# First expert's first two units in thirds of 96 rows, the second weight block on another queue, and attention's first transfers joined

## The chip, the cores and the metric

One core of a Trainium2 chip runs the whole program. The metric is the device time of one execution in microseconds (us), the median of several runs. The engines are PE (matrix products, with its weight loads shown as PEld), DVE (vector work), ACT (activations and copies), POOL (GpSimd, here mostly for splitting weights and for issuing transfers) and SP (which only issues transfers). Each of them works through its own instructions in a fixed order and waits where an instruction's inputs or buffers aren't ready.

## The reference

```python
# attention: q, k, v are [4, 8, 576, 64]
scores = where(0 <= i - j < 64, q @ k.T / 8, -1e9)
x = softmax(scores) @ v                      # taken as x [2304, 512]
# mixture of 8 experts, 288 tokens each
order = argsort(-(x @ w_gate).flatten())     # 2304 * 8 logits
for idx in order:                            # greedy: a token goes to the best
    tok, e = idx // 8, idx % 8               # expert that has room for it
    if assigned[tok] < 0 and counts[e] < 288: assign(tok, e)
for e in range(8):
    y[assigned == e] = relu(x[assigned == e] @ w1[e]) @ w2[e]   # 512 -> 1024 -> 512
# dense layer: 512 -> 2048 -> 512
out = leaky_relu(y @ w_in, 0.01) @ w_out
```

## The kernel before

**Three stages share one instruction stream per engine.** `attention` (from L60) works through 18 blocks of 128 tokens: a mask product (L121) and the products of queries and keys (L130) into one accumulator, row maxima (L137), exponentials (L145), transposes (L150), products with the values (L165), and the gate logits (L93). Its first transfers go out one after another at the start: keys, queries, the transposed values for the gate, each by SP (L86, called from L203 to L223), and the constants by ACT's queue: the mask `maskb` (L1427), the 128 columns of `cbt` that the mask product multiplies with (L1428), and the identity `ident` (L1430). The gate's weights `wg_sb` go by SP (L1431).

`Router` finds each expert's 288 tokens. It is a chain of DVE steps and of small PE products (`rp<-r_oh,r_G`, 18 in a round, with one product by `r_sel` ahead and one by `pow` behind), phase 0 for the first expert. `Moe` then runs the experts: `gather_x` fetches an expert's 288 rows in three indirect transfers of 96 rows, issued by POOL; `xtrans(n, a)` turns one such third on PE (4 transposes, `xtp<-ident,xg`) and copies it to the tile `xT`; `hstep(i)` makes the products of one of eight units of the expert (`h<-xT,w_raw`, 4 products over 288 rows) and a relu on ACT (`hh<-h`); `ystep(i)` multiplies that with the second weights into accumulators (`ya<-hh,w_raw`). The first expert runs in plain float32, where one product shows as two records in the profile; the others run in two reduced parts. A unit's weights are one block of 512 KB (`w_raw` for the first expert), loaded by `load_raw`.

`Convert` prepares the dense layer's weights on the side. They lie in memory in an 8-byte form, as units `cv_in0` to `cv_in31` of 512 KB, and pass through four buffers `cv_in` in turn. Of each unit ACT makes `cv_r<-cv_in`, `cv_in<-cv_in` and `cv_in<-cv_r`, and a join on DVE (`cv_r<-cv_r,cv_in`) ends it; only then is the buffer free, and SP issues the next unit's transfer into it.

**What sets the order.** The program is written once, front to back, but the router's pieces and the conversions are put in between by a planner. `Clocks` keeps an estimated time for every engine, queue and tile; `RouteDriver.tick` and `until` ask it, at each place where they are called, which pieces of side work look ready by that estimate, and write these there. The result is a fixed order on every engine. All of these instructions are recorded through one helper, so they carry one line number (L1286), and the names of their tiles tell them apart.

**The place of the change** is the passage from the router to the first expert in `Moe.run` (from L1075). When the first expert's tokens are known, SP loads weight block 0 (`known`). POOL then issues the three gathers, weight block 1, the transfer of the conversion's unit 6, and weight blocks 2 to 7 (L1093 to L1099). PE runs 11 products on constants (`warm`) while the rows come in, then for each third the transposes and ACT's copy, with 4 further `warm` products behind the first third and 3 behind the last; then unit 0's four products over 288 rows (`hstep(0)`), and the loop over units.

Of the kernel before, what the change touches and what calls it, by code (L numbers as in the profile page):

```python
# [6 lines left out]
F32 = mybir.dt.float32  # L7
F32R = mybir.dt.float32r
BF = mybir.dt.bfloat16
# [31 lines left out]
def lay_wg(w):  # L41
    t = np.zeros((2, 64, 4, 2, 16), np.float32)
    for h in range(2):
        t[h, :, :, h, :8] = w.reshape(4, 2, 64, 8)[:, h].transpose(1, 0, 2)
    return t.reshape(128, 4, 32)
MW = 512
# [12 lines left out]
def attention(nc, tc, ident, identb, qT, kT, v, vT, wg_sb, maskb, xd, L, filler, early, late, done):  # L59


    with ExitStack() as ctx:
# [6 lines left out]
        def load_q(n):  # L69
            qb[n] = big.tile([128, 12, 64], F32, tag="aq", name=f"aq{n}", bufs=NQ)  # L70
            pend.append((qb[n].rearrange("p j c -> p (j c)"), qT[n]))
        def load_k(b, part):
            if part == 0:
                kb[b] = big.tile([128, 10, 4, 64], F32, tag="ak", name=f"ak{b}", bufs=2)
            c0, c1 = ((0, 4, 8, 10), (0, 5, 9, 10))[b % 2][part:part + 2]
            pend.append((kb[b][:, c0:c1].rearrange("p b u c -> p (b u c)"), kT[b, :, c0:c1].rearrange("p b u c -> p (b u c)")))
# [131 lines left out]
        early()  # L208
        load_q(1)
        load_k(0, 1)  # L210
# [68 lines left out]
def consts_np():  # L279

    f, i, b = {'ident': np.eye(128, dtype=np.float32)}, {}, {}
# [521 lines left out]
WARM = 11, 4, 3  # L803
class Moe:
    def __init__(self, nc, tc, ctx, ident, pp_misc, pa, pp, w12, wsp, xd, out, route):
# [12 lines left out]
        self.seq = seq  # L818
        self.raw, self.w, self.h, self.xg, self.xT, self.acc, self.ereg, self.ph, self.hdone = {}, {}, {}, {}, {}, {}, {}, {}, {}
# [78 lines left out]
    def xtrans(self, n, a):  # L898
        nc = self.nc
# [13 lines left out]
        if n == 0:  # L913
            nc.scalar.copy(hi[:, a].bitcast(F32), pt)
            return
# [4 lines left out]
    def hprod(self, i, hi):  # L920
# [3 lines left out]
        lo = self.hdone.get(i, 0)  # L924
        self.hdone[i] = hi
# [149 lines left out]
    def run(self):  # L1075
# [3 lines left out]
        def known():  # L1079
            self.conv.hold = True  # L1080
            self.load_raw(0)
# [12 lines left out]
        self.load_raw(1, nc.gpsimd)  # L1094
# [10 lines left out]
        warm(WARM[0])  # L1105
        self.split(0, 0)
        self.split(1, 0)
        self.split(0, 1)
        for a in range(3):
            R.until(nc.done(self.xg[0, a]))  # L1110
            self.xtrans(0, a)
            if a == 0:
                warm(WARM[1])
        R.until(nc.at["tensor"] + 600)
        warm(WARM[2])
# [254 lines left out]
def build(nc, tc, qT, kT, v, vT, wg, cfd, cid, cbd, w12, wio, out):  # L1370
    with ExitStack() as ctx:
# [3 lines left out]
        ident = c.tile([128, 128], F32, name="ident")  # L1375
        cft = c.tile([128, CFN - 128], F32, name="cft")
        cit = c.tile([128, CIN], I32, name="cit")
        cbt = c.tile([128, CBN - MW], BF, name="cbt")
        cf = {k: cft[:, o - 128:o - 128 + n] for k, (o, n) in CFO.items()}
        ci = {k: cit[:, o:o + n] for k, (o, n) in CIO.items()}  # L1380
        cb = {k: cbt[:, o - MW:o - MW + n] for k, (o, n) in CBO.items()}
        ones = c.tile([128, 128], BF, name="ones"); nc.vector.memset(ones, 1.0)

        nc.scalar.activation(ident[:, 0:1], ones[:, 0:1], AF.Exp)
# [39 lines left out]
        with tc.tile_pool(name="mk", bufs=1) as mk:  # L1424
            maskb = mk.tile([128, MW], BF, name="maskb")
            wg_sb = mk.tile([128, 4, 32], F32, name="wg_sb")
            nc.scalar.dma_start(maskb, cbd[:, :MW].bitcast(BF))  # L1427
            nc.scalar.dma_start(cbt[:, :128], cbd[:, MW:MW + 128].bitcast(BF))  # L1428
            def early():
                nc.scalar.dma_start(ident, cfd[:, :128])  # L1430
                nc.sync.dma_start(wg_sb, wg)  # L1431
            def late():
                nc.sync.dma_start(cit, cid)
                nc.sync.dma_start(cft, cfd[:, 128:])
                nc.sync.dma_start(cbt[:, 128:], cbd[:, MW + 128:].bitcast(BF))
                rt.start()
            attention(nc, tc, ident, cb['ident'], qT, kT, v, vT, wg_sb, maskb, xd, L, filler, early, late, done)
# [39 lines left out]
```

## Time and profile before

| | |
|---|---|
| time, median of 3 runs | 764.27 us (764.12 to 764.67) |
| the profiled execution's own time | 765.58 us |
| its span in the trace | 763.9 us |
| granted TensorE clock over the span | 0.984 of full speed |
| PE busy | 730.4 us, 96% of the span |
| PE weight loads busy | 616.5 us, 81% |
| DVE busy | 439.0 us, 57% |
| ACT busy | 338.3 us, 44% |
| POOL busy | 170.8 us, 22% |
| bytes moved by transfers | 138.55 MB, mean 181 GB/s |

The profile shows one execution, 1.31 us longer than the median, so sums made in its rows are carried over to the median as differences. Busy shares are means over three different stages: in 40 equal slices of the span PE is below nine tenths only in the first (start), in the fourth to the sixth (end of attention, and the router's first pick), and in the last. In the timeline a row gives a start, a length, the engine, the operation, and in square brackets the idle time ahead of it and what ended that; rows of one kind that follow each other are joined, with their count behind an x. In the rows of windows each engine has its busy time and its number of instructions, then come the mean granted clock, the busy share of the transfer engines, and GB/s.

### The profile page before, as it was taken

What the parts mean: (1) busy time and instruction counts of PE and PEld (TensorE: products, weight loads), DVE (VectorE), ACT (ScalarE), POOL (GpSimd) and SP (SyncE); (2) the same over time, 40 slices, a digit from 0 to 9 for tenths busy, and PEclk for the clock granted to TensorE, in tenths of its full rate; (3) what the DMA queues carried; (4) which work ended last, traced back from release to release, by engine and by line L of the source; (5) the groups of instructions that cost most, each with busy time, mean ns of one, the idle gap of its engine ahead of it and who ended that gap; (6) DMA issues with size and microseconds to landing.
All of it is one profiled execution on the core that took longest, in us unless ns stands there. A gap on an engine that the chain in (4) does not pass through costs nothing.

```text
span 763.9 us, 14821 instructions
## 1 busy us (share of the span) xinstructions
PE 730.4 (96%) x5680; PEld 616.5 (81%) x5681; DVE 439.0 (57%) x1120; ACT 338.3 (44%) x761; POOL 170.8 (22%) x263
## 2 busy tenths in 40 slices
PE   6989659999999999999999999999999999999996
PEld 4767537898877799977778899888889998888995
DVE  3798887888988896966659623322233232222332
ACT  4888806687766444422222454312245532222221
POOL 6262130500100052010000488000038830000201
PEclk9999769999999999999999999999999999999998
DMA  9996148733784654361324464533426462324652
GB/s 351 416 415 268 56 130 309 258 112 143 269 307 178 238 187 149 105 231 56 138 84 166 143 192 155 181 110 116 158 93 216 139 223 80 111 97 166 233 191 86
DMA packets 40088, 138.55 MB, mean 181 GB/s; under 512 B 4943, under 2 KB 5967, under 8 KB 40017
## 3 DMA queue, kind: packets, MB, share of 16 engines
q1 hardware_dynamic: 34992, 122.16, 44.6%
q0 software_dynamic: 4592, 15.21, 5.8%
q8 instruction: 45, 0.74, 0.4%
q10 hardware_dynamic: 432, 0.23, 0.1%
q14 instruction: 27, 0.21, 0.1%
HBM read 117.66 MB, written 19.92 MB: 180 GB/s over the span
## 4 chain that ended last, share of the span: by engine, by line
PE 90%; DVE 7%; ACT 1%; issue 1%; DMA 1%; POOLq 0%; POOL 0%; DVEq 0%; ACTq 0%
PE h L1286 40%; PE oa L1286 26%; PE ya L1286 14%; PE rp L1286 3%; PE ao L165 2%; PE apt L150 1%; PE as L130 1%; DVE r_G L1286 1%; DVE amx L137 1%; PE xtp L1286 1%; DMA cbt<-in_cb_dram 1%; PE rq L1286 1%; PE ag L93 1%; PE as L121 0%; DVE ax L181 0%
## 5 line engine op out<-in xcount | busy, mean ns | idle before, releaser
L1286 PE MATMUL h<-Y,w 128*128 128x512 f32 (+1 forms) x600 | 135.6, 372 | 0.0
L1286 PE MATMUL oa<-w,hh 128*128 128x512 f32 x540 | 133.5, 393 | 0.0
L1286 DVE SCALAR_TENSOR_TENSOR h<-h,tg 128x512 f32<-128x512 f32 (+1 forms) x80 | 51.6, 644 | 126.5 <-ACT tg L1286 126.1
L1286 ACT COPY tg<-h 128x512 f32<-128x512 f32 (+1 forms) x80 | 43.7, 547 | 171.3 <-PE h L1286 161.5
L1286 PEld LDWEIGHTS h<-Y,w 128*128 128x128 f32 x600 | 104.0, 189 | 18.3
L1286 PEld LDWEIGHTS oa<-w,hh 128*128 128x128 f32 x540 | 99.5, 188 | 19.7
L1286 POOL TENSOR_TENSOR w<-raw,w 128x512 fp32r<-128x512 f32 x50 | 63.0, 1292 | 194.2 <-ACT w L1286 193.9
L1286 PE MATMUL h<-xT,w 128*128 128x288 f32 x672 | 100.8, 297 | 0.1
L1286 PE MATMUL ya<-hh,w 128*128 128x288 f32 x672 | 100.4, 297 | 0.0
L1286 PEld LDWEIGHTS h<-xT,w 128*128 128x128 f32 x672 | 92.6, 188 | 0.9 <-DVE xT L1286 0.3
L1286 PEld LDWEIGHTS ya<-hh,w 128*128 128x128 f32 x672 | 92.1, 188 | 0.2 <-DVE hh L1286 0.2
L1286 PE MATMUL h<-Y,res 128*128 128x512 f32 (+1 forms) x360 | 84.4, 376 | 0.0
L1286 PE MATMUL oa<-res,hh 128*128 128x512 f32 x324 | 82.5, 399 | 0.0
L1286 DVE TENSOR_TENSOR hh<-h,hh 128x512 fp32r<-128x512 f32 (+1 forms) x80 | 51.0, 637 | 36.2 <-ACT hh L1286 33.4
L1286 ACT CAST hh<-h 128x512 fp32r<-128x512 f32 (+1 forms) x80 | 43.6, 545 | 62.9 <-DVE h L1286 62.4
L1286 POOL DMA_INDIRECT out_dram<-ot,sidx x18 | 22.5, 1251 | 218.2 <-DVE ot L1286 215.2
L1286 PEld LDWEIGHTS h<-Y,res 128*128 128x128 f32 x360 | 61.8, 188 | 11.3
L1286 PEld LDWEIGHTS oa<-res,hh 128*128 128x128 f32 x324 | 59.4, 188 | 13.3 <-ACT hh L1286 0.5
L1286 ACT ACTIVATE hh<-h 128x288 fp32r<-128x288 f32 (+1 forms) x64 | 26.6, 416 | 85.7 <-PE h L1286 78.0
L1286 ACT CAST w<-raw 128x512 fp32r<-128x512 f32 x112 | 64.2, 621 | 0.0
L1286 DVE SCALAR_TENSOR_TENSOR hh<-h,hh 128x288 fp32r<-128x288 f32 x56 | 25.5, 455 | 65.5 <-ACT hh L1286 62.0
L145 ACT ACTIVATE ap<-as,anm 128x128 f32<-128x128 f32 x144 | 42.0, 405 | 18.0 <-DVE anm L138 11.5
(177 smaller groups left out, 935.1 us busy)
## 6 DMA issues: line engine op xcount, KB each, us to landing
w<-wsp SPq DMA_DIRECT2D x80, 512.0 KB
raw<-in_w_dram SPq DMA_DIRECT2D x53, 512.0 KB
cv_in<-in_wio_dram SPq DMA_DIRECT2D x31, 512.0 KB
wsp<-w SPq DMA_DIRECT2D x20, 512.0 KB
avo<-in_v_dram SPq DMA_DIRECT2D x6, 876.0 KB
aq<-in_q_dram SPq DMA_DIRECT2D x12, 384.0 KB
avt<-in_vt_dram SPq DMA_DIRECT2D x6, 768.0 KB
xd<-ax SPq DMA_DIRECT2D x18, 256.0 KB
```

The source lines that it names most:

```text
L93: nc.tensor.matmul(ps[32 * u:32 * u + 32, :], wg_sb[:, u, :], vtb[m][:, u, :], start=True, stop=True, skip_group_check=True)
L130: nc.tensor.matmul(S[64 * t:64 * t + 64, a, u, :].rearrange("p (b c) -> p b c", b=2), q[h], k[h], start=False, stop=True, skip_group_check ...
L137: nc.vector.tensor_reduce(out=mx, in_=S[:, a:a + n], axis=AX.X, op=ALU.max)
L145: nc.scalar.activation(p[:, u, :], S[:, a, u, :], AF.Exp, bias=nm[a][:, u:u + 1], scale=0.125)
L150: nc.tensor.transpose(pt[:, u, :], p[:, u, :], ident)
L165: nc.tensor.matmul(o[64 * t:64 * t + 64, h // 4, h % 4, :], ptb[:, u, 64 * t:64 * t + 64], (ve, vo)[t][m][:, s, h, :], start=True, stop=Tr ...
L1286: return f(*a, **kw)
```

## The change

- **Attention's start.** Identity and gate weights come as one array `iwg` of 256 columns, in one transfer on ACT's queue; mask and the 128 constant columns of the mask product come as one tile and one transfer. SP's transfer of the gate weights is gone, and the second part of the first keys is issued ahead of the second queries.
- **Weight blocks 0 and 1** are both issued by SP in `known`; POOL's transfer of block 1 is gone.
- **Warm products.** The 4 and the 3 further ones are gone, the 11 stay.
- **Thirds.** The products of units 0 and 1 are no longer made over 288 rows at once. `third(i, a)` makes unit i's four products over the 96 rows of third a, as soon as these are turned: (0,0), (1,0) behind the second transposes, then after the third transposes (0,1), (1,1), (0,2), (1,2). ACT copies each third to a place of its own (`xF`), which the products read; for the first two thirds DVE copies the same transposes to `xT`, which the other six units read.

```diff
     t = np.zeros((2, 64, 4, 2, 16), np.float32)
...
-    return t.reshape(128, 4, 32)
+    return np.concatenate([np.eye(128, dtype=np.float32), t.reshape(128, 128)], 1)
...
         early()
+        load_k(0, 1)
         load_q(1)
-        load_k(0, 1)
...
-WARM = 11, 4, 3
+WARM = 11
...
         if n == 0:
-            nc.scalar.copy(hi[:, a].bitcast(F32), pt)
+            if a < 2:
+                x = lo if a == 0 else self.wk.tile([128, 2, 512], F32R, tag="hh", name="xF1")
+                self.xF[a] = x.bitcast(F32)[:, 0] if a == 0 else x.rearrange("p a n -> p (a n)").bitcast(F32)[:, :384].rearrange("p (k c) -> p k c", k=4)
+                nc.scalar.copy(self.xF[a], pt)
+                nc.vector.tensor_copy(hi[:, a].bitcast(F32), pt)
+            else:
+                nc.scalar.copy(hi[:, a].bitcast(F32), pt)
+                self.xF[a] = hi.bitcast(F32)[:, a]
             return
...
         lo = self.hdone.get(i, 0)
+        if lo == 12:
+            return
...
             self.conv.hold = True
-            self.load_raw(0)
+            for i in range(2):
+                self.load_raw(i)
...
         self.gather_x(0)
-        self.load_raw(1, nc.gpsimd)
...
-        warm(WARM[0])
+        warm(WARM)
...
+        def third(i, a):
+            if a == 0:
+                self.ph[i] = self.pp.tile([128, 512], F32, tag="h", name=f"h{i}")
+                self.hdone[i] = 12
+            for k in range(4):
+                nc.tensor.matmul(self.ph[i][:, 96 * a:96 * a + 96], self.w[i, 0][:, 128 * k:128 * k + 128], self.xF[a][:, k], start=(k == 0), stop=(k == 3), skip_group_check=True)
         for a in range(3):
             R.until(nc.done(self.xg[0, a]))
             self.xtrans(0, a)
-            if a == 0:
-                warm(WARM[1])
-        R.until(nc.at["tensor"] + 600)
-        warm(WARM[2])
+            if a < 2:
+                third(a, 0)
+        for i, a in ((0, 1), (1, 1), (0, 2), (1, 2)):
+            third(i, a)
+            R.tick()
         self.hstep(0)
...
-            nc.scalar.dma_start(maskb, cbd[:, :MW].bitcast(BF))
-            nc.scalar.dma_start(cbt[:, :128], cbd[:, MW:MW + 128].bitcast(BF))
+            maskb = mk.tile([128, MW + 128], BF, name="maskb")
+            nc.scalar.dma_start(maskb, cbd[:, :MW + 128].bitcast(BF))
...
             def early():
-                nc.scalar.dma_start(ident, cfd[:, :128])
-                nc.sync.dma_start(wg_sb, wg)
+                nc.scalar.dma_start(iwg, wg)
```

Since the planner's estimates move with the change, the order of side work moves too. Three places of it follow. In the names, `h0` and `h1` are the accumulators of units 0 and 1, `hh0` and `hh1` what the relu makes of them, `cv_in7` and `cv_r7` the conversion's unit 7 (read and made), and `rp` the router's products for the second expert.

On ACT, from the copies of the first expert's rows on, before:

```order
L1286 COPY xT0_0_2190<-xtp0_2_2231 128x384
L1286 ACTIVATE hh0_2280<-h0_2246 128x288
L1286 ACTIVATE cv_r6_2304<-cv_in6_2144 128x512
L1286 ACTIVATE cv_in6_2144<-cv_in6_2144 128x512
L1286 ACTIVATE hh1_2318<-h1_2282 128x288
L1286 CAST res_2_73<-cv_in4_1193 128x512
L1286 CAST res_3_74<-cv_in5_1196 128x512
L1286 ACTIVATE cv_in6_2144<-cv_r6_2304 128x512
L1286 ACTIVATE cv_r7_2379<-cv_in7_2269 128x512
```

and with the change:

```order
L1303 COPY xF1_2209<-xtp0_1_2204 128x384
L1303 COPY xT0_0_2187<-xtp0_2_2237 128x384
L1303 ACTIVATE cv_r7_2253<-cv_in7_2248 128x512
L1303 ACTIVATE hh0_2271<-h0_2196 128x288
L1303 ACTIVATE hh1_2273<-h1_2212 128x288
L1303 CAST res_2_73<-cv_in4_1190 128x512
L1303 ACTIVATE cv_r6_2301<-cv_in6_2132 128x512
```

The first activation of conversion unit 7 stood behind both relus and behind unit 6; now it stands ahead of them all, directly behind the copy of the last third.

On DVE, from the router's large r_G steps on, before:

```order
L1286 TENSOR_TENSOR r_G0_127<-r_m_1_2177,cit_64 128x6x127 x3
L1286 SCALAR_TENSOR_TENSOR r_E_1_0_2203<-r_M_122 128x18
L1286 SCALAR_TENSOR_TENSOR r_sat_126<-rp16_2211,ones_66 127x8
L1286 SCALAR_TENSOR_TENSOR r_G1_128<-r_E_1_0_2203,rp17_2238,cft_63 128x18x31
L1286 SCALAR_TENSOR_TENSOR r_E_1_1_2241<-r_E_1_0_2203,rp17_2238,r_M_122 128x18
L1286 SCALAR_TENSOR_TENSOR cv_r3_1781<-cv_r3_1781,cv_in3_1009 128x512
```

and with the change:

```order
L1303 TENSOR_TENSOR r_G0_127<-r_m_1_2174,cit_64 128x6x127 x2
L1303 COPY xT0_0_2187<-xtp0_0_2189 128x384
L1303 TENSOR_TENSOR r_G0_127<-r_m_1_2174,cit_64 128x6x127
L1303 SCALAR_TENSOR_TENSOR r_E_1_0_2202<-r_M_122 128x18
L1303 COPY xT0_0_2187<-xtp0_1_2204 128x384
L1303 SCALAR_TENSOR_TENSOR cv_r3_1778<-cv_r3_1778,cv_in3_1006 128x512
L1303 SCALAR_TENSOR_TENSOR r_sat_126<-rp16_2217,ones_66 127x8
```

The join of unit 3, behind which SP issues the transfer of unit 7, stood behind one router round (`r_sat`, `r_G1`, `r_E_1_1`); now it stands ahead of that round and behind the two new copies.

On PE, from the last transposes to the first product with the second weights, with the change:

```order
L1303 MATMUL xtp0_2_2237<-iwg_62,xg2_0_2130 128x96 x4
L1303 MATMUL h0_2196<-xF1_2209,w_raw0_2084 128x96 x4
L1303 LDWEIGHTS pow2_0_90
L1303 MATMUL rp17_2251<-r_sat_126,pow2_0_90 128x8
L1303 MATMUL h1_2212<-xF1_2209,w_raw1_2086 128x96 x4
L1303 MATMUL h0_2196<-xT0_0_2187,w_raw0_2084 128x96 x4
L1303 MATMUL h1_2212<-xT0_0_2187,w_raw1_2086 128x96 x4
L1303 MATMUL ya0_0_2275<-hh0_2271,w_raw0_2084 128x288
```

Before, `warm` and unit 0's four products over 288 rows followed the last transposes, with two rounds of the router's 18 products between the products of units 0 and 1; now nothing stands between the last third and `ya0`, and those two rounds come behind it.

## Rows read from the trace of the kernel before

**Rows 1.** The page's chain of work that ended last, by engine.
```profile
PE 90%; DVE 7%; ACT 1%; issue 1%; DMA 1%; POOLq 0%; POOL 0%; DVEq 0%; ACTq 0%
```
**Rows 2.** Windows: us, then PE, PEld, DVE, ACT, POOL busy, PEclk, DMA share, GB/s.
```profile
112.40:150.00 37.60, 37.60 (x294) 29.05 (x293) 30.46 (x88) 21.74 (x37) 11.30 (x26) 1.00 0.81 296
112.00:122.00 10.00, 10.00 (x111) 7.32 (x110) 7.48 (x17) 5.27 (x10) 1.16 (x3) 1.00 1.02 399
```
**Rows 3.** Waits of PE from 112.4 us to the end: total, times, longest.
```profile
PE rp L1286 <- ACT r_cq L1286: 0.8, 2, 0.6
```
**Rows 4.** Timeline of PE, 102 to 126 us: start, length, instruction.
```profile
108.63 0.52 PE L1286 MATMUL xtp<-ident,xg 96*128 96x96 f32 x4
108.99 1.03 PE L1286 MATMUL warm<-cbt 128*128 128x512 bf16 x4
...
113.03 0.59 PE L1286 MATMUL rp<-r_oh,r_G 128*128 128x8 bf16 x18
113.48 0.73 PE L1286 MATMUL h<-xT,w_raw 128*128 128x288 f32 x2
...
117.79 0.65 PE L1286 MATMUL ya<-hh,w_raw 128*128 128x288 f32 x2
```
**Rows 5.** Timeline of ACT, 102 to 126 us.
```profile
109.24 0.48 ACT L1286 COPY xT<-xtp 128x384 f32<-128x384 f32 x1 [13.76 <-PE xtp L1286]
...
115.33 0.41 ACT L1286 ACTIVATE hh<-h 128x288 f32<-128x288 f32 x1 [2.97 <-PE h L1286]
115.64 0.69 ACT L1286 ACTIVATE cv_r<-cv_in 128x512 f32<-128x512 f32 x1
...
121.40 0.69 ACT L1286 ACTIVATE cv_r<-cv_in 128x512 f32<-128x512 f32 x1 [0.65 <-DMA cv_in<-in_wio_dram]
```
**Rows 6.** Timeline of DVE, 102 to 126 us.
```profile
108.42 2.67 DVE L1286 TENSOR_TENSOR r_G<-r_m,cit 128x762 bf16<-128x762 f32 x3
111.01 0.17 DVE L1286 SCALAR_TENSOR_TENSOR r_E<-r_M 128x18 f32<-128x18 int32 x1
...
112.80 0.68 DVE L1286 SCALAR_TENSOR_TENSOR cv_r<-cv_r,cv_in 128x512 int32<-128x512 int32 x1
```
**Rows 7.** Timeline of SP's queue, 102 to 126 us: transfers issued.
```profile
102.76 0.36 SPq L1286 DMA_DIRECT2D w_raw<-in_w_dram  x1
113.51 10.58 SPq L1286 DMA_DIRECT2D cv_in<-in_wio_dram  x4
```
**Rows 8.** Timeline of POOL, 102 to 126 us: its last transfers issued.
```profile
110.00 3.17 POOL L1286 DMA_DIRECT2D w_raw<-in_w_dram  x6
```
**Rows 9.** Windows of 1 us, columns as in rows 2.
```profile
85.00:86.00 1.00, 0.00 (x0) 0.00 (x0) 0.93 (x4) 1.00 (x3) 0.00 (x0) 1.00 0.00 0
...
87.00:88.00 1.00, 0.27 (x4) 0.19 (x4) 0.82 (x4) 1.00 (x7) 0.00 (x0) 0.58 0.00 0
...
104.00:105.00 1.00, 0.66 (x19) 0.51 (x17) 0.24 (x1) 0.00 (x0) 0.00 (x0) 0.50 0.68 221
...
106.00:107.00 1.00, 1.00 (x4) 0.38 (x3) 0.87 (x4) 0.00 (x0) 0.70 (x2) 0.50 0.00 0
107.00:108.00 1.00, 1.00 (x5) 0.39 (x4) 0.97 (x6) 0.00 (x0) 0.69 (x2) 0.68 0.72 188
```
**Rows 10.** Groups of weight loads by line and form: busy, mean ns, idle before.
```profile
L1286 PEld LDWEIGHTS h<-xT,w_raw 128*128 128x128 f32 x64 | 11.4, 190 | 3.4 <-issue 0.4 <-ACT xT L1286 0.4
...
L93 PEld LDWEIGHTS ag<-avt,wg_sb 128*32 128x32 f32 x48 | 1.0, 113 | 3.5 <-ACT aptb L152 3.2 <-DMA avt<-in_vt_dram 0.3
```
**Rows 11.** Timeline of the first 12 us: ACT's queue, PE, PEld.
```profile
1.20 0.40 ACTq L1427 DMA_DIRECT2D maskb<-in_cb_dram  x1
1.63 0.45 ACTq L1428 DMA_DIRECT2D cbt<-in_cb_dram  x1
...
6.19 0.64 PE L121 MATMUL as<-maskb,cbt 64*64 64x512 bf16 x4 [6.19 <-DMA cbt<-in_cb_dram]
...
10.95 0.20 PEld L93 LDWEIGHTS ag<-avt,wg_sb 128*32 128x32 f32 x8 [0.33 <-DMA avt<-in_vt_dram]
```

More of the change, by code (lines that the diff above doesn't have):

```diff
@@ L279, in consts_np @@
 def consts_np():
-    f, i, b = {'ident': np.eye(128, dtype=np.float32)}, {}, {}
+    f, i, b = {}, {}, {}
     p = np.arange(128, dtype=np.float32)[:, None]
@@ L818, in __init__ @@
         self.seq = seq
+        self.xF = [None] * 3
         self.raw, self.w, self.h, self.xg, self.xT, self.acc, self.ereg, self.ph, self.hdone = {}, {}, {}, {}, {}, {}, {}, {}, {}
@@ L1374, in build @@
         dr = ctx.enter_context(tc.tile_pool(name="dr", bufs=1, space=bass.MemoryType.DRAM))
-        ident = c.tile([128, 128], F32, name="ident")
-        cft = c.tile([128, CFN - 128], F32, name="cft")
+        iwg = c.tile([128, 256], F32, name="iwg")
+        ident = iwg[:, :128]
+        cft = c.tile([128, CFN], F32, name="cft")
         cit = c.tile([128, CIN], I32, name="cit")
-        cbt = c.tile([128, CBN - MW], BF, name="cbt")
-        cf = {k: cft[:, o - 128:o - 128 + n] for k, (o, n) in CFO.items()}
+        cbt = c.tile([128, CBN - MW - 128], BF, name="cbt")
+        cf = {k: cft[:, o:o + n] for k, (o, n) in CFO.items()}
         ci = {k: cit[:, o:o + n] for k, (o, n) in CIO.items()}
-        cb = {k: cbt[:, o - MW:o - MW + n] for k, (o, n) in CBO.items()}
+        cb = {k: cbt[:, o - MW - 128:o - MW - 128 + n] for k, (o, n) in CBO.items() if o > MW}
         ones = c.tile([128, 128], BF, name="ones"); nc.vector.memset(ones, 1.0)
-        nc.scalar.activation(ident[:, 0:1], ones[:, 0:1], AF.Exp)
+        nc.scalar.activation(iwg[:, 0:1], ones[:, 0:1], AF.Exp)
         L = c.tile([128, 160], F32, name="L")[:, :NT * 8].rearrange("p (c e) -> p c e", e=8)
@@ L1424, in build @@
         with tc.tile_pool(name="mk", bufs=1) as mk:
-            maskb = mk.tile([128, MW], BF, name="maskb")
-            wg_sb = mk.tile([128, 4, 32], F32, name="wg_sb")
-            nc.scalar.dma_start(maskb, cbd[:, :MW].bitcast(BF))
-            nc.scalar.dma_start(cbt[:, :128], cbd[:, MW:MW + 128].bitcast(BF))
+            maskb = mk.tile([128, MW + 128], BF, name="maskb")
+            nc.scalar.dma_start(maskb, cbd[:, :MW + 128].bitcast(BF))
+            wg_sb = iwg[:, 128:].rearrange("p (u e) -> p u e", u=4)
             def early():
-                nc.scalar.dma_start(ident, cfd[:, :128])
-                nc.sync.dma_start(wg_sb, wg)
+                nc.scalar.dma_start(iwg, wg)
             def late():
                 nc.sync.dma_start(cit, cid)
-                nc.sync.dma_start(cft, cfd[:, 128:])
-                nc.sync.dma_start(cbt[:, 128:], cbd[:, MW + 128:].bitcast(BF))
+                nc.sync.dma_start(cft, cfd)
+                nc.sync.dma_start(cbt, cbd[:, MW + 128:].bitcast(BF))
                 rt.start()
-            attention(nc, tc, ident, cb['ident'], qT, kT, v, vT, wg_sb, maskb, xd, L, filler, early, late, done)
+            attention(nc, tc, ident, maskb[:, MW:], qT, kT, v, vT, wg_sb, maskb, xd, L, filler, early, late, done)
         pa = ctx.enter_context(tc.tile_pool(name="m_pa", bufs=4, space=PSUM, reuse_waits="tile"))
```

## The prediction

> **What bounds the kernel now.** Read the chain of work that ended last first: PE carries 90% of it [rows 1]. A share is a mean, so the next view is the windows. From 112.4 to 150 us PE is busy for all of its 37.60 us at full clock, with ACT at 21.74 and DVE at 30.46 us beside it [rows 2], and the table of waits says that this goes on: from 112.4 us to the end PE waits for another engine twice, 0.8 us in all [rows 3]. So whatever moves the point at which the first expert is under way moves the end by as much, and nothing behind it can take a delay up. What the change touches lies ahead of 112.4 us or directly behind it; the questions are when PE can begin `ya` (unit 0's second product), and with how much of the other work already done.
>
> Before, that product begins at 117.79 [rows 4]. By then PE has also done two router rounds that the change puts behind it. A round's 18 products put off the product behind them by 113.48 - 113.03 = 0.45 us [rows 4]; with the one by r_sel and the one by pow I take 0.5, so the two are 1.0 and the mark to compare with is 117.79 - 1.0 = **116.8**.
>
> **The change part by part.**
>
> *Thirds.* 16 records of 288 columns become 48 of 96, in six thirds of 8. No row has this product. The nearest is the transposes of the same 96 columns: four, and the next instruction begins 108.99 - 108.63 = 0.36 later [rows 4], so 90 ns a record. The other end is a limit by the weight load: a load of 32 columns takes 113 ns and one of 128 takes 190 [rows 10], a slope of 0.80 ns a column, so 103 ns for 128 columns. I take 90 (same columns) and keep 103. Third (0,0) can start when ACT's copy ends, 109.24 + 0.48 = 109.72 [rows 5]. Then 0.72 for a third, 0.36 for the transposes: (0,0) ends at 110.5, the second transposes at 110.8, (1,0) at 111.55, the router's group at 112.05, the third transposes at 112.4, (0,1) at 113.1, then the product by pow, which waits for DVE (below) until 113.15, (1,1) at 113.9, (0,2) at 114.65, (1,2) at **115.4**; at 103 ns it is 116.0. The relu of unit 0 (0.41, [rows 5]) fits beside (1,2). Standing alone, this part gives 1.4 us, or 0.8.
>
> *ACT's new order.* But the relu isn't next on ACT: the first activation of conversion unit 7 now stands ahead of both relus, and it waits for a transfer. That transfer goes into the buffer of unit 3, so SP issues it only when DVE's join of unit 3 has ended: before, the join ran from 112.80 for 0.68 [rows 6], and the issue stood at 113.51 [rows 7]. ACT got the data at 121.40, having waited 0.65 us for it with nothing else to do [rows 5]: 7.9 us for 512 KB. The reason is in the windows: from 112 to 122 us the transfer engines are 1.02 busy at 399 GB/s [rows 2], because POOL issued six weight blocks from 110.00 to 113.17 [rows 8] (block 1 and unit 6 lie ahead of them in its queue). Before, that lateness cost nothing, since both relus stood ahead; with the change PE's `ya` stands behind the relu, the relu behind the activation, and the activation behind this transfer.
>
> When is the issue now? DVE's three r_G steps take 0.89 each from 108.42 [rows 6]; the first copy to `xT` goes in behind the second, the second behind r_E. I price a copy at 0.48, as ACT's of the same tile [rows 5]; the other end is 0.68, the join of 512 columns [rows 6]. That puts the third r_G's end at 111.6, r_E's at 111.75 and the second copy's at 112.3, the join's at **113.0** and the issue with it (113.2 at the dear price), and the router's next step just behind. One block less is in POOL's queue, since block 1 goes by SP, right behind block 0. If the transfer lands when the whole backlog is through, one block less is 524 KB / 399 GB/s = 1.3 us off the 121.36 of before: 120.05. If it takes 7.9 us again, 120.9. I take the middle, **120.4**. The lowest price is that of a block with the engines to itself: block 0, issued at 102.76 [rows 7], and the engines idle in 106 to 107 [rows 9], so in by 106.0, 3.24 us, which would be 116.2.
>
> From 120.4 on: activation 0.69, relu 0.41 [rows 5], and 0.1 for the two handovers, so `ya` starts at **121.6**. Against 116.8 that is **+4.8 us**. PE has its last third behind it at 115.4 to 116.0 and nothing in its order to fill the gap: five to six us idle.
>
> *The clock in that gap.* The trace has one such gap: PE is busy 0.00 in 85 to 86, and the granted clock falls in 87 to 88 to a mean of 0.58 [rows 9], that is, to the lower level (0.50, 1.2 GHz) for most of it. Coming back, PE is at work again in 104 to 105 (0.66 busy, clock 0.50), and the clock rises in 107 to 108: a mean of 0.68 puts it at 107.64 [rows 9], 2.6 to 3.6 us later. I expect a fall inside the gap, and 2.8 us of work at half pace behind it: half of that, **+1.4**. Bounds: 0, if it stays; 2.8, if it takes twice as long to return.
>
> *Attention's start.* PE's first instruction waits until 6.19 for `cbt`, whose transfer is issued at 1.63, 0.43 behind the mask's at 1.20 [rows 11]. Joined, the bytes can land up to 0.43 sooner. But the gate's first load still waits 0.33 us at 10.95 for values that lie behind the same bytes [rows 11], and these don't shrink. Bounds -0.43 and 0; I take **-0.2**.
>
> *At nothing.* The 7 `warm` products run where PE waits anyway, and the thirds take their place as work that keeps the clock up. DVE's two copies matter only by the join's date, counted above. Weight block 1 on SP begins beside block 0 in a stretch at 0.68 of the engines' time [rows 9] and is needed at 110.8, so up to 0.3 on the gathers, covered by the gap. Router rounds run later, with the same wait as cover; were that gone, their 1.0 is already in the mark of 116.8.
>
> **Sum.** 4.8 + 1.4 - 0.2 = +6.0. The profiled execution's own time, 765.58, becomes 771.6; the median lies 1.31 below it, so the forecast for the median is 764.27 + 6.0 = **770.3**.
>
> **The rivals.**
>
> *The same stall, clock stays up.* For it: PE is busy until the gap at full clock, and the gap is shorter than the thin stretch behind 85 us. Against: the clock fell there some 2 us after PE stopped. 764.27 + 4.8 - 0.2 = 768.9.
>
> *Queues take turns.* If SP's queue got half of the engines as soon as it has work, unit 7 would need the 3.24 us of a lone block plus once more its own 1.3 us: in at 117.55, `ya` at 118.75, +1.95 - 0.2, the gap too short for the clock: 766.0. The trace speaks against it, since with a backlog of this kind the transfer took 7.9 us. The Trainium skill's page "DMA: Bandwidth & Descriptors", section "Queues, rings and completion order", states this rule (each engine goes round the queues that have work, a packet at a time); the 7.9 us don't agree with equal shares.
>
> *Not slower: unit 7 lands as a lone block would.* With one block less in POOL's queue and unit 6 first in it, the backlog might be thin at 113.0. In at 116.2, `ya` at 117.4, +0.6 - 0.2: 764.7. The point that decides: the sum stays within 0.2% if `ya` starts by 118.5, so if unit 7 lands by 117.3. For it: block 0's 3.24 us. Against: even with block 1 gone, the six blocks behind it were issued in the 3 us just ahead.
>
> *Faster: ACT is not held at all.* If unit 7 is in by 114, or the activation isn't where the order has it, the thirds bring their 1.4 at 90 ns, and with the start's 0.2 it is 762.7; at 103 ns 763.3, which is no change. Landing 1 us after its issue is against every row.
>
> **How the numbers follow.** A measurement of this kernel can tell about 0.2%, 1.53 us: faster is below 762.74, slower above 765.80. Chances: forecast 0.60; stall without the clock 0.20; taking turns 0.05; lone block 0.10; ACT not held 0.05. The first three are slower, 0.85; the fourth no change, 0.10; the last faster, 0.05. Range: up, the dear copies and 120.9 for the landing (+0.7) and a slower return of the clock, of which I take in most, 772.9. Down, it goes through the stall without the clock (768.4 at the early landing) and taking turns to 766.0. That leaves out the last two rivals, 0.15, and a little above.
>
> **What would show it.** Right: on ACT, `cv_r<-cv_in` directly ahead of the first `hh`, released by a transfer near 120.4 after some 7 us of idle; PE idle from about 115.5 to 121.6; the granted clock at 0.50 in a window behind that, products there at twice their length; the thirds' records at 90 to 103 ns. Wrong: that transfer landing by 117 (first step of the ACT part), a first `ya` ahead of 118.5, a gap on PE that another instruction fills, or a clock of 1.00 through the gap; and a delay that doesn't reach the end, which would mean that PE has slack behind 150 us that the waits don't show.

## The result, and the profile after

The changed kernel takes **771.11 us** (median of 6 runs, 770.33 to 772.66), against 764.47 (764.12 to 764.95, 6 runs) for the kernel before on the same chip: 1.009 times, 95% interval 1.0077 to 1.0103, or 6.6 us slower. Forecast were 770.3 and a range of 766.0 to 772.9. The profiled execution is the shortest of the six (770.33, span 768.7), so its rows show a loss of 4.7 against the span of before, and 1.9 us of the median's 6.6 are not in them: 0.8 because it is the shortest, 1.1 because the one of before was long.

ACT's timeline after the change (start, length, instruction, idle ahead of it and what ended that; this holds for all timelines below) answers to [rows 5]:

```profile
112.41 0.48 ACT L1303 COPY xT<-xtp 128x384 f32<-128x384 f32 x1 [1.26 <-PE xtp L1303]
119.15 0.66 ACT L1303 ACTIVATE cv_r<-cv_in 128x512 f32<-128x512 f32 x1 [6.26 <-DMA cv_in<-in_wio_dram]
119.71 0.69 ACT L1303 ACTIVATE hh<-h 128x288 f32<-128x288 f32 x2
```

The activation of unit 7 stands directly behind the third copy, waits 6.26 us for its transfer, and both relus come out behind it. DVE and SP, as [rows 6, 7]:

```profile
109.63 0.94 DVE L1303 TENSOR_TENSOR r_G<-r_m,cit 128x762 bf16<-128x762 f32 x1
110.49 0.17 DVE L1303 SCALAR_TENSOR_TENSOR r_E<-r_M 128x18 f32<-128x18 int32 x1
111.19 0.56 DVE L1303 COPY xT<-xtp 128x384 f32<-128x384 f32 x1 [0.53 <-ACT xF L1303]
111.66 0.68 DVE L1303 SCALAR_TENSOR_TENSOR cv_r<-cv_r,cv_in 128x512 int32<-128x512 int32 x1
```

```profile
112.37 0.34 SPq L1303 DMA_DIRECT2D cv_in<-in_wio_dram  x1
```

From issue to the activation it is 119.15 - 112.37 = 6.78 us. PE, as [rows 4]:

```profile
109.18 1.13 PE L1303 MATMUL h<-xT,w_raw 128*128 128x96 f32 x8 [0.61 <-ACT xT L1303]
110.14 0.49 PE L1303 MATMUL xtp<-iwg,xg 96*128 96x96 f32 x4
110.48 1.06 PE L1303 MATMUL h<-xT,w_raw 128*128 128x96 f32 x8
...
114.08 1.95 PE L1303 MATMUL h<-xT,w_raw 128*128 128x96 f32 x16
120.16 1.33 PE L1303 MATMUL ya<-hh,w_raw 128*128 128x288 f32 x2 [4.12 <-ACT hh L1303]
...
123.00 2.08 PE L1303 MATMUL ya<-hh,w_raw 128*128 128x288 f32 x4
124.92 0.65 PE L1303 MATMUL h<-xT,w_raw 128*128 128x288 f32 x2
```

PE has its last third behind it at 116.03 and waits 4.12 us. Then the first two records of `ya` (one product) take 1.33 us, where [rows 4] has 0.65. The windows of that stretch (columns as in [rows 2]) say why:

```profile
117.00:118.00 1.00, 0.00 (x0) 0.00 (x0) 0.00 (x0) 0.00 (x0) 0.00 (x0) 0.97 1.03 422
118.00:119.00 1.00, 0.00 (x0) 0.00 (x0) 0.00 (x0) 0.00 (x0) 0.00 (x0) 0.50 1.04 422
...
123.00:124.00 1.00, 1.00 (x4) 0.82 (x3) 0.79 (x2) 0.98 (x1) 0.00 (x0) 0.50 0.00 0
124.00:125.00 1.00, 1.00 (x4) 0.70 (x3) 1.00 (x4) 0.00 (x0) 0.00 (x0) 0.62 0.04 8
```

The granted clock falls to its lower level at 117.9, two us into the gap, and is back at 124.8 (0.62 in the last window), so PE works 4.6 us at 1.2 GHz. From the first `ya` to the next unit's first product it takes 124.92 - 120.16 = 4.76 us. All this time the transfer engines are full at 422 GB/s until the backlog is through.

How unit 7's transfer lands is told by the packets of the queues (`q0` is POOL's queue, `q1` SP's; packets, MB, share of the 16 transfer engines): first from its issue at 112.37 to its first packet at 115.88, then 115.9 to 118.4 us, then 118.8 to 122:

```profile
q0 software_dynamic: 373, 1.36, 100.2%
...
q0 software_dynamic: 146, 0.53, 52.2%
q1 hardware_dynamic: 130, 0.51, 50.1%
...
q0 software_dynamic: 200, 0.69, 52.7%
```

For 3.5 us nothing of it moves; then it gets as much as the backlog, 0.51 MB against 0.53; and it is through with 0.69 MB of the backlog still to come. The last weight block, issued at 111.03 and so ahead of it, lands at 122.0, behind it. In all twelve profiles with the weight blocks ahead of it (all but c2's, below) the first packet comes 3.4 to 3.6 us after the issue, and POOL's queue moves 1.25 to 1.46 MB in that time. What the transfer waits for then isn't shown.

The waits of PE from 112.4 us to the end (total, times, longest), as [rows 3]:

```profile
PE ya L1303 <- ACT hh L1303: 4.1, 1, 4.1
PE oa L1303 <- ACT hh L1303: 0.2, 1, 0.2
```

Nothing behind takes the delay up. The start, PE's timeline as [rows 11], and one row of before for the gate's products:

```profile
4.88 0.64 PE L121 MATMUL as<-maskb 64*64 64x512 bf16 x4 [4.88 <-DMA maskb<-in_cb_dram]
...
10.75 0.85 PE L93 MATMUL ag<-avt,iwg 128*32 128x384 f32 x8 [0.76 <-DMA avt<-in_vt_dram]
```

```profile
10.96 1.37 PE L93 MATMUL ag<-avt,wg_sb 128*32 128x384 f32 x8
```

The first product starts 1.31 sooner, the gate 0.21 sooner, and its eight records take 0.85 where they took 1.37: the first record of the granted clock in the trace, at 1.00, begins at 8.7 us here and at 12.1 before.

For what follows, one table read from PE's timelines of all profiled executions: **a** is the start of the router's last large group ahead of the first expert (`rp<-r_lo,r_OB`), **b** goes from a to the first `ya`, **c** from a to the start of the first expert's last `ya` record, **d** from that to the end of the span. The sum a + c + d is the end.

| kernel | a | b | c | d |
|---|---|---|---|---|
| before | 103.80 | 13.99 | 45.98 | 614.10 |
| changed | 102.74 | 17.42 | 52.32 | 613.54 |
| a1, units 6 to 8 held | 102.80 | 13.55 | 45.98 | 618.52 |
| a2, gap filled | 102.53 | 18.39 | 51.29 | 614.46 |
| a3, start alone | 102.80 | 13.99 | 45.98 | 613.05 |
| a4, start and block 1 | 102.64 | 14.15 | 46.14 | 613.20 |
| c1, activation behind relus | 103.33 | 12.77 | 50.21 | 614.44 |
| c2, less backlog | 102.67 | 15.01 | 47.92 | 613.56 |
| c3, before with the stall | 103.64 | 19.39 | 53.34 | 613.45 |
| c4, planner with one stream | 102.86 | 13.72 | 46.69 | 622.84 |
| c5, activation further back | 103.33 | 13.84 | 46.67 | 615.89 |
| d1, 96 columns in place | 103.69 | 15.36 | 47.37 | 613.86 |
| e1, thirds in before's order | 103.36 | 14.98 | 47.69 | 614.13 |

In the profile the change makes a shorter by 1.06, c longer by 6.34 and d shorter by 0.56. So all that is lost is lost within the first expert, and in the trace it is the gap and the slow products behind it. Whether the thirds have a part in it, the trace alone doesn't say.

### The profile page after: what moved, and what is told of

It reads as the page before. It is cut to its first block, busy times and chain, and to the rows that moved or that the text cites. A ratio compares the mean times of both kernels' runs of the same rounds, so it can differ in the third digit from the quotient of the medians.

```text
span 768.7 us, 14869 instructions
## 1 busy us (share of the span) xinstructions
PE 732.2 (95%) x5706; PEld 619.1 (81%) x5706; DVE 440.3 (57%) x1124; ACT 337.1 (44%) x761; POOL 165.6 (22%) x260
## 4 chain that ended last, share of the span: by engine, by line
PE 89%; DVE 7%; DMA 1%; ACT 1%; issue 1%; POOLq 0%; POOL 0%; SPq 0%; DVEq 0%; ACTq 0%
PE h L1303 39%; PE oa L1303 26%; PE ya L1303 14%; PE rp L1303 2%; PE ao L165 2%; PE as L130 1%; PE apt L150 1%; DVE amx L137 1%; PE xtp L1303 1%; DVE r_G L1303 1%; DMA cv_in<-in_wio_dram 1%; DMA aq<-in_q_dram 1%; PE warm L1303 1%; PE rq L1303 1%; ACT ap L145 1%
## 5 line engine op out<-in xcount | busy, mean ns | idle before, releaser
L1303 POOL DMA_INDIRECT out_dram<-ot,sidx x18 | 18.9, 1050 | 310.0 <-DVE ot L1303 134.7
L1303 POOL TENSOR_TENSOR w<-raw,w 128x512 fp32r<-128x512 f32 x48 | 60.4, 1295 | 95.4 <-ACT w L1303 95.0
L1303 POOL DMA_INDIRECT xg<-xd,r_ids x24 | 24.1, 1005 | 127.5 <-issue 48.6
```

The costliest lines, as they stand in the source:

```text
L1303: return f(*a, **kw)
```

## The experiments

The theory: one instruction, unit 7's activation ahead of the first relu, holds PE until a transfer lands, and the clock falls meanwhile. The rival: the thirds cost it (reloaded weights, DVE's copies, the order that comes with them), and the activation is only where the wait shows.

**a1: conversions held back.**

```diff
-                if n < 32 and (self.left[n] if n in self.out else ...
+                if n < 32 and n not in self.skip and (self.left[n] if n in self.out else ...
...
+        self.conv.skip = {7, 8}
...
+            if i == 1:
+                self.conv.skip = set()
```

> The changed kernel with one thing undone: ACT may not begin conversion units 6, 7 and 8 ahead of the first relu (6 may run behind it, 7 and 8 behind the second), so the activation that waits for unit 7's transfer stands behind both relus again. Stall theory: PE's gap of 4.1 us ahead of the first ya goes, and with it the 2.2 us that the first ya group lost at half clock (4.76 us from its first product to the next unit's, against 2.61 before): some 6.5 us less than the changed kernel in one profile, and against the kernel before the 1.06 us of the earlier start less what the thirds cost (120 ns a record in the trace of the change: they end 0.3 later than the mark 116.8 - 1.06): 763.7. Rival (the thirds' reloads, block 1 beside the gathers or DVE's copies are the cost, and the activation is only where the wait shows): another wait takes its place and the time stays above 768.

Measured: 767.73 (767.23 to 769.13; before 764.75; 1.0042, 1.0028 to 1.0055), neither 763.7 nor above 768. Ahead of the first relu `skip` is {6, 7, 8}. The gap is gone (b 13.55) and the first expert ends at 45.98, exactly as before; but d is 618.52. The planner, asked at other moments, laid out the rest anew, and PE meets waits there that neither kernel has (waits of PE in a1):

```profile
PE rp L1306 <- ACT r_cq L1306: 2.1, 1, 2.1
PE ya L1306 <- DVE hh L1306: 0.7, 1, 0.7
```

So 767.7 says nothing on the thirds: the edit changed more than it meant to. The runs c1, c2, c3 and c5 therefore move instructions behind the planner's back: it is told of them in the old place, and every other instruction keeps its order.

**a2: warm products in the gap.**

```diff
             R.tick()
+        for _ in range(16):
+            nc.tensor.eng.matmul(wt, self.warm[:, :128], self.warm, start=True, stop=True)
         self.hstep(0)
```

> The changed kernel, with 16 warm products (0.22 us each, 3.5 us in all) on PE behind the last third, in the gap; the gap's end stays set by unit 7's transfer. Clock theory: the granted clock stays at 1.00, the first ya group takes 2.6 us in place of 4.8, and the time falls by 2.2 to some 768.9; the stall of 4.4 us stays. Rival (the long products come from contention or from something else that ends with the transfer): no change against the changed kernel, 771.1.

Measured: 770.55 (769.6 to 772.6; 1.0085, 1.0069 to 1.01), only 0.6 below the change. PE and ACT in its profile:

```profile
115.47 3.40 PE L1134 MATMUL warm<-cbt 128*128 128x512 bf16 x15
120.91 0.75 PE L1305 MATMUL ya<-hh,w_raw 128*128 128x288 f32 x2 [2.04 <-ACT hh L1305]
...
123.63 0.65 PE L1305 MATMUL h<-xT,w_raw 128*128 128x288 f32 x2
```

```profile
119.91 0.66 ACT L1305 ACTIVATE cv_r<-cv_in 128x512 f32<-128x512 f32 x1 [7.62 <-DMA cv_in<-in_wio_dram]
```

The first `ya` group takes 123.63 - 120.91 = 2.72 us in place of 4.76, so the clock's part is 2.0 us, as the theory had it: the granted clock stays at 1.00 here. But the transfer, issued at 111.76, took 8.15 us here against 6.78, which gives 1.4 back in these two profiles. The landing varies between executions; that fits the wider runs here (3 us from lowest to highest) and in the change (2.3, against 0.9 in a3), though c3's four runs, which wait for it too, lie within 1.1. In the medians the clock's part is thus not separated from that.

**a3: the start alone**, the change's edits to the constants and attention's transfers and no others.

> The kernel before with attention's start alone from the change (identity with gate weights, mask with its constants, keys ahead of queries). If the 1.06 us by which the router's last products stood earlier in the profile of the change are all from here and reach the end: 763.4. If the gate's wait takes them back, as the prediction had it: 764.3.

Measured: 763.97 (763.53 to 764.39, 11 runs; before 764.75; 0.9992, 0.9983 to 1.0001): 0.8 gained in the medians, between the two expectations; the interval just takes in no change. In its profile a is 1.00 shorter.

**a4: start and block 1 on SP**, as a3, and with SP issuing weight block 1 and conversions held as in a1; units 0 and 1 over 288 rows.

> As the first run of this set, but with units 0 and 1 as products over 288 rows as before, and the 4 and 3 further warm products: what is left of the change is the start and block 1 on SP. Stall theory: 763.4, like the start alone (block 1 on SP is worth nothing by itself). The difference of the first run of this set to this one is the thirds' own price: +0.3 by the 120 ns a record of the profile; -0.8 to -1.4 by the 90 to 103 ns of the prediction.

Measured: 763.87 (763.3 to 764.64, 11 runs; 0.9989, 0.998 to 0.9998), like a3: block 1's queue and the held conversions are worth nothing that these runs can tell. The comparison with a1 fails, as a1's d shows.

**c3: the stall alone, in the kernel before.** One instruction is moved:

```diff
+        if i == 0:
+            self.conv.pre = self.conv.room(7)
+            nc.scalar.eng.activation(self.conv.pre, self.conv.st[7][:, :, 1].bitcast(F32), AF.Copy, scale=float(2.0 ** -112))
         if kind == "e" and n == 0:
             nc.scalar.activation(hi.bitcast(F32), ph[:, :N], AF.Relu)
```

> The kernel before with one instruction moved: the first activation of unit 7 stands ahead of the first relu on ACT, nothing else of the change. Stall theory: ACT gets the data at 121.4 as before, the relu ends at 122.4, ya starts at 122.5 in place of 117.8 (+4.7) and the clock falls in a gap of 4.8 us (+2.2): 764.75 + 6.9 = 771.6, all of the change's loss and its 0.8 gain at the start. Rival (the thirds are needed for the loss): +4.7 at the most, 769.5 or less.

Measured: **771.88** (771.01 to 772.12; before 764.6; 1.009, 1.0075 to 1.0104). ACT and PE in its profile:

```profile
122.02 0.66 ACT L974 ACTIVATE cv_r<-cv_in 128x512 f32<-128x512 f32 x1 [9.17 <-DMA cv_in<-in_wio_dram]
122.58 0.39 ACT L1292 ACTIVATE hh<-h 128x288 f32<-128x288 f32 x1
```

```profile
117.22 1.22 PE L1292 MATMUL h<-xT,w_raw 128*128 128x288 f32 x4
123.03 1.33 PE L1292 MATMUL ya<-hh,w_raw 128*128 128x288 f32 x2 [4.59 <-ACT hh L1292]
```

The old products, the old queues, the old start, and one activation in front of one relu: 7.3 us slower, with the same gap and the same slow products as in the change (c +7.36). The thirds aren't needed for a loss of this size.

**c1: that activation put back behind the two relus, in the changed kernel.**

```diff
+        if k == 0 and n == 7:
+            e, a, kw = self.nc.scalar, (o, t[:, :, 1].bitcast(F32), AF.Copy), dict(scale=float(2.0 ** -112))
+            e.clocks.charge(e.e, "activation", a, kw)
+            self.held = lambda: e.eng.activation(*a, **kw)
...
                     self.hstep(i + 1)
+                if i == 0:
+                    self.conv.held()
```

> The changed kernel with one instruction moved and every other one in its order on every engine: the first activation of unit 7 stands behind the two first relus on ACT, not ahead of them. Stall theory: no gap on PE ahead of ya, which starts at 116.1 in the profile (120.2 with the change), the clock stays up, and the gain is the stall and the clock together, 4.1 to 5.4 (the landing varied from 6.8 to 8.1 us) plus 2.2: some 764.0. Rival from the run that held unit 7 (767.7): the thirds and the order around them cost 3 to 4 us by themselves, and this run ends near 767.7 too.

Measured: 769.19 (768.45 to 770.36; 1.0058, 1.0045 to 1.0071). Missed: `ya` starts at 116.10 without a wait, but four us later PE stops again. PE, ACT and DVE:

```profile
119.71 0.73 PE L1309 MATMUL h<-xT,w_raw 128*128 128x288 f32 x2
123.46 0.17 PE L1309 MATMUL rp<-r_sat,pow 128*128 128x8 bf16 x1 [3.01 <-DVE r_sat L1309]
```

```profile
120.18 0.66 ACT L694 ACTIVATE cv_r<-cv_in 128x512 f32<-128x512 f32 x1 [3.40 <-DMA cv_in<-in_wio_dram]
120.74 0.63 ACT L1309 CAST res<-cv_in 128x512 fp32r<-128x512 f32 x1
```

```profile
118.62 0.24 DVE L1309 SCALAR_TENSOR_TENSOR r_E<-r_E,rp,r_M 128x18 f32<-128x18 f32 x1
121.40 0.69 DVE L1309 TENSOR_TENSOR res<-cv_in,res 128x512 fp32r<-128x512 f32 x1 [2.54 <-ACT res L1309]
...
123.22 0.18 DVE L1309 TENSOR_TENSOR_SCAN r_sat<-rp,ones 31x8 bf16<-31x8 f32 x1
```

The same transfer reaches PE by a second way: behind the waiting activation stand ACT's casts of units 4 and 5, behind a cast DVE's subtraction, behind that the router's `r_sat`, and behind that PE's product by `pow`, in front of the rest of unit 2.

**c5: the activation further back**, behind the third relu: as c1, but `self.held()` is called ahead of unit 7's second activation.

> The changed kernel with the first activation of unit 7 moved further back than in the swap: behind the third relu, directly ahead of unit 7's second activation, all else in its order. In the swap PE's gap came back at 120.4, three us long, because ACT's casts for units 4 and 5 stood behind the waiting activation, DVE's subtraction behind the cast and the router's r_sat behind that. Stall theory, with that second way named: no gap over 0.5 us ahead of 125, the clock stays up, the first expert ends at 148.8 as with the start alone (155.06 with the change, so -6.3), and the order of the change behind it stands 0.5 better than before's: 763.3 to 764.8. Rival (the order around the thirds loses 3 to 4 us wherever the activation stands): 767 or more.

Measured: 767.76 (767.2 to 768.26; before 765.28; 1.0035, 1.0021 to 1.0049): 2.5 above before, where the change is 6.6 above. PE has no gap in the first expert, and c is 46.67. Waits of PE from 270 to 640 us:

```profile
PE rp L1309 <- DVE r_ip L1309: 1.5, 1, 1.5
PE rp L1309 <- DVE r_G L1309: 0.6, 1, 0.6
```

The order of the rest is that of the change, but d is 615.89, not 613.54: with PE ahead by some five us, the router's later phases are late for it, 2.1 us. So of the stall's 6.3, some 2 hide a delay that the change's order has anyway. The stall theory's 763.3 to 764.8 is missed. The rival's "767 or more" is met by the number, though its loss of 3 to 4 us isn't: the thirds and the order, less what the start gains, cost 2.5 us here without the stall, most of it in d (615.89 against 614.10 before), 0.7 in c. How much is the thirds' and how much the order's, this run doesn't tell.

**c2: less backlog.** Blocks 4 to 7 go out on SP directly behind unit 7, not on POOL ahead of it:

```diff
+            if 4 <= i < 8:
+                eng.clocks.charge(eng.e, "dma_start", (r, src(eng)), {})
+                self.conv.behind.append(lambda: nc.sync.eng.dma_start(r, src(nc.sync)))
```

> The changed kernel, but weight blocks 4 to 7 are issued by SP directly behind unit 7's transfer, not by POOL ahead of it; all else stands where it stood. Backlog theory: with two blocks fewer ahead of it the transfer lands some 3.3 to 4.6 us after its issue (6.8 to 8.2 with the backlog), ya starts by 117.2 to 118.3, the clock hardly falls: 765 to 767. Rival (a transfer of unit 7 takes 7 to 8 us by itself, for its 8-byte rows or its place on SP): no change, 771.

Measured: 768.45 (765.81 to 771.26, 7 runs; 1.0048, 1.0031 to 1.0065): 1.5 above the range of its theory in the median, and the runs spread over 5 us. SP, ACT and PE in the profile (its span, 764.2, is among the short ones):

```profile
112.97 0.34 SPq L1311 DMA_DIRECT2D cv_in<-in_wio_dram  x1
113.51 2.02 SPq L853 DMA_DIRECT2D w_raw<-in_w_dram  x4
```

```profile
116.67 0.66 ACT L1311 ACTIVATE cv_r<-cv_in 128x512 f32<-128x512 f32 x1 [3.18 <-DMA cv_in<-in_wio_dram]
```

```profile
117.68 0.75 PE L1311 MATMUL ya<-hh,w_raw 128*128 128x288 f32 x2 [1.05 <-ACT hh L1311]
```

Here the transfer takes 3.70 us, as long as block 0, with no other block under way, takes from issue to landing (3.6 us in a3, 3.7 in c3; the prediction had 3.24), and the gap is 1.05 us with the clock up. Its first packet comes 1.0 us after the issue, as POOL's queue runs dry. That it takes 7 to 8 us otherwise is thus the work of the blocks ahead of it, not of its kind or its queue. How it lands in the long runs of this kernel isn't shown.

**c4: a planner that knows of the backlog.**

```diff
-            by, end = "dma", max(self.pipe.get(e, 0), q) + n / self.RATE
-            self.pipe[e] = end
+            by, end = "dma", max(self.pipe.get(0, 0), q) + n / self.RATE
+            self.pipe[0] = end
```

> The changed kernel, but the planner reckons the transfers of all queues as one stream, not one stream for each queue; by that estimate it puts unit 7's first activation behind the third relu by itself, and the order of other side work moves throughout. Stall theory: no gap ahead of ya; how the rest of the order comes out isn't known: 763.5 to 768. Rival (the stall isn't the planner's doing): a gap of 4 us ahead of ya stays, 770 or more.

Measured: 774.35 (774.09 to 776.14; 1.0133, 1.0119 to 1.0148). The first `ya` comes 13.72 after the group, with no gap, and unit 7's activation stands behind the third relu: it was the planner's separate streams that put it in front. But d is 622.84, 9 us more; the new order makes PE wait for the router's steps in many places. Better estimates at one place didn't make a better order of the whole; which of the moved steps cost the 9 us wasn't tried apart.

**d1: the thirds' price in place.** The kernel of a3, with each of the 8 products of units 0 and 1 made as three of 96 columns, one behind the other with the same weights. Its three accumulations interleave in one bank, and `h` of these units comes out with other values than in the other kernels.

> The kernel before with attention's start (763.97 in the run of that alone), where units 0 and 1 are made in 48 products of 96 columns in place of 16 of 288, at the same place and in the same order of everything else: the price of the thirds by itself. By the 120 ns a record of the changed kernel's profile: 48 x 0.120 - 16 x 0.242 = +1.9, so 765.9. By the prediction's 90 ns: +0.4, by its 103 ns: +1.1. If the relu of unit 0 or something else covers it: +0.5 or less.

Measured: 766.24 (765.23 to 766.96, 11 runs; before 765.28; 1.0009, 1.0 to 1.0018); against a3's 0.9992 that is 0.0017, or 1.3 us. In the trace:

```profile
112.48 0.80 PE L938 MATMUL h<-xT,w_raw 128*128 128x96 f32 x6
...
119.05 0.68 PE L1292 MATMUL ya<-hh,w_raw 128*128 128x288 f32 x2
```

First product to first `ya`: 6.57 us, in the kernel before 117.79 - 112.41 = 5.38, with the same router rounds between. So 48 records cost 1.19 more than 16 of 0.242: (16 x 0.242 + 1.19) / 48 = 105 ns each, nearest to the 103 ns of the expectation (+1.1).

**e1: the thirds in the order of before**: a4 with the thirds, the copies and without the 7 warm products, the planner being told of whole products.

> The thirds without the new order: the kernel of the fourth run (attention's start and block 1 on SP; 763.87) with the thirds, ACT's copies to places of their own and DVE's two copies, but everything else (router, conversions, relus) kept in the order of before, the planner being told of the whole products; the 7 further warm products are gone. If the loss is the order alone: no gap ahead of ya, no wait behind it that wasn't there before, and the thirds are worth what the earlier start of PE's work (2.7 us) leaves after 48 records of 115 ns in place of 16 of 242 (1.6 us) and the transposes and router group that they push back: nothing to 0.7 us, so 763.2 to 764.2. If the thirds themselves lose (their reloads, DVE's copies ahead of the router's steps): 765 or more.

Measured: 766.67 (765.61 to 767.54, 11 runs; before 765.29; 1.0016, 1.0007 to 1.0025). Against a4's 0.9989 the thirds lose 0.0027, some 2 us: above my 763.2 to 764.2. In the profile c is 47.69 against 46.14: the waits of PE that the kernel before hasn't are small,

```profile
PE rp L1314 <- DVE r_E L1314: 0.5, 1, 0.5
PE rp L1314 <- DVE r_sat L1314: 0.3, 1, 0.3
```

and at 115 ns a record (the change's own) the thirds cost 48 x 0.115 - 16 x 0.242 = 1.6 us more of PE, about what c shows. They give PE work 2.3 us sooner (109.82 - 103.36 = 6.5 us behind the group a, where a4 has 111.41 - 102.64 = 8.8), but that work pushes the third transposes back (112.50 - 103.36 = 9.1, where a4 has 110.31 - 102.64 = 7.7), and nothing is left of it. How the 1.6 divides between the records and the waits isn't shown; in a1, with another order, the same thirds leave c as it was before (45.98).

## Why the prediction was right

**Direction and mechanism were right, and the size was near**: +6.0 forecast, +6.6 measured, and c3 shows that the one moved activation makes such a loss by itself (+7.3). It isn't all of the change's: with the activation out of the way (c5) 2.5 are still lost, so its removal gives back some 4.1 of the 6.6. Step by step:

- *The mark and the carry.* Right. Behind the first expert the changed kernel loses nothing (d 613.54 against 614.10). It doesn't hold for all of the five us by which c5's first expert ends sooner than the change's: 2.1 of them go in waits for the router.
- *ACT's order and the landing.* The order and the path were right, and the landing's time was met in part by luck. Taking the start's 1.06 out, the issue was at 113.4 (forecast 113.0: the second copy waited 0.53 for ACT's), the data at 120.2 (120.4), `ya` at 121.2 (121.6). The transfer took 6.8 us here, between the 7.9 and the lower bound; over the profiles with the full backlog it took 6.8 to 8.2, and one block less showed no clear effect (8.06 us in a3, where unit 7's activation also waited, 7.78 in a4). The forecast took the middle of two readings: that the transfer lands when the whole backlog is through, and that it takes 7.9 us again. The first is wrong, since it landed with 0.69 MB of the backlog still to come; the second was 1.1 us too long.
- *Queues that take turns.* As a forecast this rival failed: it would have had the data 4.55 us after the issue, and they took 6.8 to 8.2. But the prediction's reason against it, that 7.9 us don't agree with equal shares, was a misreading. From its first packet on the transfer does get an equal share (0.51 MB against 0.53 in 2.5 us), in the kernel before too (0.20 MB each from 117 to 118 us). What the rival lacked is the 3.4 to 3.6 us ahead of the first packet. The Trainium skill's page "DMA: Bandwidth & Descriptors", section "Queues, rings and completion order", states that each engine goes round the queues that have work, a packet at a time. With that these shares agree.
- *The clock.* The mechanism was right, the term was mis-sized: +1.4 forecast from 2.8 us at half pace; the clock came back only after 4.6 us of work (c3: it is at 0.50 from the first `ya` at 123.0 to past 127), and the first group took 4.76 against 2.61, +2.15. The 2.8 came from one return only, on 11 warm products. The 2.15 lies within the stated bounds of 0 and 2.8.
- *The start.* Mis-sized: -0.2, with a bound of -0.43, against -0.8 in a3 and -1.06 in the profile. The bound took the difference of two issue times for the most that joining can give, but the first product came 1.31 sooner. The gate came 0.21 sooner; then its products ran at the upper pace (0.85 against 1.37 for eight records), and this I hadn't counted. How much of that is the joined start isn't shown: c3, with the old start, has 0.89 for them (clock up at 11.3), and c1, with the joined one, 1.24 (clock up at 11.5). The 0.8 of a3 is itself at the edge of its interval.
- *The thirds.* Mis-sized: 90 ns a record taken, 103 kept as the other end; 105 in d1, and in the change 0.89 to 0.96 us for eight, some 115. They ended at 116.03, 1.7 later than 115.4 moved by the start (114.3); 0.5 of that lies ahead of the first third. Under the gap this cost nothing, which is why the total held; the rival "ACT is not held at all" is what it makes wrong, since c5 and e1 show no gain of 1.4 but a loss.
- *The rivals and the range.* The stall with the clock up is what a2 makes by filling the gap, and it isn't what the change does. The lone block's landing came only with the backlog taken away (c2). The range's upper end, 772.9, is 0.5 above what the parts named for it add to (770.3 + 0.7 + 1.4 = 772.4); the 771.1 lies below both.

The sum in the profile: -1.06, +4.4 at the first `ya` against the mark (120.16 - 115.74), +2.15 for the slow group, and -0.8 behind it (0.24 in the first expert, 0.56 in d) make the 4.7; forecast -0.2, +4.8, +1.4 and nothing. The terms miss by -0.9, -0.4, +0.75 and -0.8, partly against each other. The forecast is 1.3 above these rows and 0.6 below the medians, so that the total came so close is in part luck.

Of all versions a4 is the fastest: 763.87, 0.9989 of before (0.998 to 0.9998). That is attention's joined start with block 1 on SP and no thirds; a3, without block 1 there, is level with it (763.97).

## What to carry to other kernels

Before an instruction is allowed ahead of the one that the busiest engine waits for, ask what ends its own wait; a transfer issued beside a backlog on another queue took 6.8 to 8.2 us here in place of 3.7. It neither lands as if alone nor has to wait for the whole backlog, so read from the packets of each queue when it begins to move and what share it gets. Look for everything that is queued behind the waiting instruction, on every engine: c1 took the first way away and the same wait came through DVE. And an order that a planner has written is a whole: an edit that made it lay out the rest anew lengthened what follows the first expert by 5 us (a1) and 9 us (c4) here, so an experiment on one instruction has to keep the others where they were.

## What the runs showed of the hardware that wasn't expected

- In c1 the clock did not fall within PE's gap of 3 us (123.46 ends it); it fell after PE had taken up work again, and PE worked at half pace until past 127:

```profile
122.00:123.00 1.00, 0.00 (x0) 0.00 (x0) 0.59 (x2) 1.00 (x2) 0.00 (x0) 1.00 0.16 66
123.00:124.00 1.00, 0.54 (x3) 0.49 (x3) 0.71 (x3) 0.97 (x2) 0.00 (x0) 1.00 0.83 164
124.00:125.00 1.00, 1.00 (x4) 0.67 (x4) 1.00 (x3) 0.43 (x1) 0.00 (x0) 0.55 0.85 344
```

- The same 512 KB on the same queue took 3.7 us in one kernel and 6.8 to 8.2 in others, and in c2's profile the four blocks issued right behind it on its own queue did not hold it up. Most of the difference lies ahead of its first packet, which comes 1.0 us after the issue in c2 and 3.4 to 3.6 in all others.
- The stretch ahead of the first expert differs by up to 1.2 us between profiles with the same code there (a from 102.53 to 103.69 among those with the joined start), so a gain of that size at the start is read from medians, not from one profile. The clock's rise at the start differs as well: with PE's first product at 4.9 to 5.2 us in all eleven profiles with the joined start, the first record of the clock at 1.00 begins anywhere from 8.5 to 11.5.
